# Attention forward of a memory-segment transformer block: softmax sums moved into the score banks, V's far heads copied straight from PSUM, and a reordered store of V and P

## The chip, the cores and the metric

One core of a Trainium2 chip. The metric is device time in microseconds (us), median of several runs. Engines by their names in the profile: PE (TensorE: matmuls; its weight loads are PEld), ACT (ScalarE), DVE (VectorE), POOL (GpSimd) and SP (SyncE, which here issues DMAs; its instruction queue is written SPq).

## The reference

The kernel computes the output of a transformer block and all of its gradients. The part that matters here is the forward of the attention with memory: 2048 rows of 512 are cut into 64 segments of 32 rows, and each segment is attended together with 8 memory rows, which are the first 8 output rows of the segment before. So the 64 steps are sequential.

```python
for s in range(n_seg):
    xs = x[:, s * seg_len:(s + 1) * seg_len, :].copy()
    h = jnp.concatenate([mem, xs], axis=1)
    q = jnp.einsum('btd,dhe->bhte', h, Wq)
    k = jnp.einsum('btd,dhe->bhte', h, Wk)
    v = jnp.einsum('btd,dhe->bhte', h, Wv)
    scores = jnp.einsum('bhqe,bhke->bhqk', q, k) * scale
    scores = jnp.where(mask[None, None], scores, -1000000000.0)
    p = _softmax(scores, axis=-1)
    o = jnp.einsum('bhqk,bhke->bhqe', p, v)
    o = jnp.einsum('bhte,hed->btd', o, Wo)
    mem = o[:, :M, :].copy()
    outs.append(o[:, M:, :])
```

There are 32 heads of 128. After the attention come a gated feed-forward part and the backward of everything, for which the forward stores Q, K, V, the normalised P and the head outputs O of every step.

## The kernel before

The forward is `phase2`, a Python loop over `s` that is unrolled into one program; `s4 = s % 4`. Its instructions are written in order, and `self.pin` keeps that order on each engine, so what an engine does next is the order of the text.

The loop treats 32 rows per step: the 8 memory rows and the first 24 rows of the segment. The last 8 rows of four segments together (the *tails*) are projected as one block of 32 rows, ahead of time (`b_pieces`: RBk, RBq, RBv), and stored at s4 = 1 (RBk) and 2 (RBq). One step runs so:

- Projections of K, Q and V (`col_pass`, L255): each in two halves of 16 heads. Four column groups of TensorE work at once, so the result of a half lies as 128 partitions (4 x 32 rows) by 512: the heads 24 to 31 in partitions 96 to 127. They are copied out of PSUM to RA (L61 on ACT, L63 on DVE). `turns` transposes K and Q by TensorE to the layout kT, qT.
- V has to go to the *head layout* Vst: 11 groups of 3 heads, 32 rows each in partitions 0 to 95, tail rows in 96 to 119 (`v_tails`, by DMA from RBv). GpSimd copies partitions 0 to 95 of each half (L794, L797). The heads of partitions 96 to 127 have to move to other partitions: `vshift` (L740) does it with three products with the identity, and DVE copies the result (L743).
- `st_exp`, three parts of 4, 4 and 3 head groups: scores of a group (L715) are added to a mask that `mask_mm` (L664) has put in the bank (pool `pst`, three banks), and ACT takes the exponential of a part into ET (L717).
- `den` (L721) multiplies ET by a column of ones, the softmax sums; the sums of all parts lie in the last quarter of the bank or2. `pv` (L750) multiplies ET by V. `recip` (L726) and `ost` (L759 ACT, L762 DVE) divide, giving Ost. As part 2's product goes to or2 as well, it comes after the reading of the first sums.
- `ott` (L733) transposes Ost by TensorE to OT, `outproj` (L223) multiplies by Wo; the two halves of the sum are split, folded (L240), and the memory columns become the next step's hT (L875), on which its projections of K wait.

Between these, `slots` and `mod_r` hold side work: turning RBk or RBq (s4 = 2, 3), projecting tails, a 128-column piece of the modulation (mostly s4 = 0), the next layernorm tile.

SP issues the stores and two DMA transpositions per step: VTr from Vst (L814), and Pst from ET (L820), each with a single buffer. P is scaled by GpSimd (`norm`, L885), and VT and PS are stored (L887, L888) in the step after, by the call at its very start. Ost and OT are stored to OSR and OT (L858, L869), the rows of K and Q to KST and QST (L589, L590). All go through one queue of SP in the order of the text.

Of the kernel before, what the change touches and what calls it, by code (L numbers as in the profile page):

```python
# [10 lines left out]
ALU = mybir.AluOpType  # L11
# [29 lines left out]
class K:  # L41
# [392 lines left out]
    def phase2(self):  # L434
        nc, tc, cfg, io = self.nc, self.tc, self.cfg, self.io
        D, DC, H, E, L, M, T, G, NS = cfg.D, cfg.DC, cfg.H, cfg.E, cfg.L, cfg.M, cfg.T, cfg.G, cfg.NS
        GW = 128
        NP = 3
        PG = 4
# [8 lines left out]
        with ExitStack() as ctx:  # L448
# [10 lines left out]
            def ps_f32(name):  # L459
                return psp.tile([128, PG, GW], F32, name=name, tag="p")  # L460
# [92 lines left out]
            def part3(t, pi):  # L553
                return t[:, pi * PW:min((pi + 1) * PW, G * GW)].rearrange("p (g x) -> p g x", x=GW)
# [7 lines left out]
            Ws = {"q": Wq, "k": Wk, "v": Wv}  # L562

            def pass_half(x, hf, lhs, rows, eng):
                self.col_pass(psp, Ws[x], hf, lhs, rows, eng)

            def turn_half(rows, hf):
                return self.turn_half(psp, rows, hf)
# [74 lines left out]
            def fill(s4, where):  # L643
                for f in slots.pop((s4, where), []):
                    f()
# [14 lines left out]
            def mask_mm(pi):  # L660

                n = min(PG, G - pi * PG)
                ps = masked[pi] = pst.tile([128, PG, GW], F32, name="st_ps", tag="st")
                nc.tensor.matmul(ps[:, 0:n, 0:120], lhsT=self.ident[:, :], rhs=maskT[:, 0:n, :], start=True, stop=False,  # L664
                                 skip_group_check=True)
# [15 lines left out]
            for s in range(NS):  # L681
# [10 lines left out]
                def proj(x, hf, eng):  # L692
                    pass_half(x, hf, lambda c: hT[:, c, :], RA[x], eng)
                    if hf == 1 and x != "v" and s < NS - 1:
                        rows_out(RA[x], DR[x], s, 1)
# [5 lines left out]
                def turns():  # L701
                    tps = []
                    for x in "kq":
                        for hf in range(2):
                            tps.append((x, hf, ("act", "dve")[hf], turn_half(RA[x], hf)))
                            to_heads(tps[-1][2], XT[x], tps[-1][3][:], 4 * hf, 4, 32, 0, far=False)
                    for x, hf, eng, tp in tps:
                        to_heads(eng, XT[x], tp[:], 4 * hf, 4, 32, 0, own=False)

                def st_exp(pi):  # L710
                    st_ps = masked.pop(pi)
                    n = min(PG, G - pi * PG)
                    for j in range(n):
                        g = pi * PG + j
                        nc.tensor.matmul(st_ps[:, j, 0:120], lhsT=x120(KT, g), rhs=QT[:, g * 120:g * 120 + 120],  # L715
                                         start=False, stop=True, skip_group_check=True)
                    nc.scalar.activation(part3(ET, pi)[:, 0:n, 0:120], st_ps[:, 0:n, 0:120], AF.Exp, scale=cfg.scale)  # L717

                def den(pi, ps):
                    for g in range(pi * PG, min(pi * PG + PG, G)):  # L720
                        nc.tensor.matmul(ps[:, PG - 1, g:g + 1], lhsT=ET[:, g * GW:(g + 1) * GW], rhs=self.ones[:, 0:1],  # L721
                                         start=True, stop=True)

                def recip(a, b, ps):
                    a, b = a * PG, min(b * PG, G)
                    nc.vector.reciprocal(rden[:, a:b], ps[0:120, PG - 1, a:b])  # L726

                def transposes_part(src, pi, w=GW):
                    ps = ps_b16("tps")
# [3 lines left out]
                        nc.tensor.transpose(ps[:, j, :], src[:, g * w:g * w + GW], self.ident[:, :])  # L733
                    return ps[:, 0:n, :], n

                def vshift():
                    sh = ps_f32("sh_ps")
                    shf = sh[:].rearrange("p g x -> p (g x)")
                    for hl in range(3):
                        nc.tensor.matmul(shf[32 * hl:32 * hl + 32, 0:384], lhsT=self.ident[96:128, 96:128],  # L740
                                         rhs=RA["v"][96:128, 384 * hl:384 * hl + 384], start=True, stop=True,
                                         tile_position=(96, 32 * hl))
                    nc.vector.tensor_copy(Vst[0:96, 1024:1408], shf[0:96, 0:384])  # L743

                def pv(pi, or_ps=None):
                    or_ps = or_ps or ps_f32("or_ps")
                    n = min(PG, G - pi * PG)
                    for j in range(n):
                        g = pi * PG + j
                        nc.tensor.matmul(or_ps[:, j, :], lhsT=ET[:, g * GW:(g + 1) * GW], rhs=Vst[:, g * GW:(g + 1) * GW],  # L750
                                         start=True, stop=True)
                    return or_ps

                def ost(pi, or_ps, eng):
                    n = min(PG, G - pi * PG)
                    if eng == "act":
                        for j in range(n):
                            g = pi * PG + j
                            nc.scalar.activation(Ost[0:120, g * GW:(g + 1) * GW], or_ps[0:120, j, :], AF.Copy,  # L759
                                                 scale=rden[:, g:g + 1])  # L760
                        return
                    nc.vector.tensor_tensor(part3(Ost, pi)[0:120, 0:n, :], or_ps[0:120, 0:n, :],  # L762
                                            rden[:, pi * PG:pi * PG + n].unsqueeze(2).to_broadcast([120, n, 128]), op=ALU.mult)

                def ott(pi):
                    ps, n = transposes_part(Ost, pi)
                    self.evac("dve" if pi == 1 else "act", part3(OT, pi)[:, 0:n, :], ps)

                def outproj():
                    ps = psp.tile([128, 256], F32, name="at_ps", tag="p")  # L770
# [3 lines left out]
                        self.pair_mm(ps, [OT[:, off(h):off(h) + 32] for h in hs], [Wo[:, h, :] for h in hs], n, H // 2)  # L774
                    return ps

                if s < NS - 1 and norms:
                    norms.pop()()
                proj("k", 0, "dve")
                proj("k", 1, "act")  # L780
                if s == NS - 1:
                    nc.gpsimd.dma_start(self.w_gate, io["B_w_gate"].rearrange("(c p) f -> p c f", p=128))
                    norms.pop()()
                if s == 0:
                    for f in firsts["k"]:
                        f()
# [5 lines left out]
                    tails_in("kq", 0)  # L792
                proj("v", 0, "dve")
                nc.gpsimd.tensor_copy(Vst[0:96, 0:512], RA["v"][0:96, 0:512])  # L794
                turns()
                proj("v", 1, "dve")
                nc.gpsimd.tensor_copy(Vst[0:96, 512:1024], RA["v"][0:96, 512:1024])  # L797
                if s == 0:
                    for f in firsts["v"]:
                        f()  # L800
# [7 lines left out]
                    late_rows()  # L808
                st_exp(0)
                st_exp(1)  # L810
                vshift()
                st_exp(2)
                if s < NS - 1:
                    nc.sync.dma_start(VTr[:], Vst[:, :], transpose=True)  # L814
                or2 = ps_f32("or_ps")
                den(0, or2)
                or0 = pv(0)
                Pst = sb2.tile([128, G, 128], BF16, name="Pst", bufs=1)
                if s < NS - 1:
# [1 line left out]
                else:  # L821
                    nc.gpsimd.dma_start(self.w_up, io["B_w_up"].rearrange("(c p) f -> p c f", p=128))
                    nc.gpsimd.dma_start(self.w_down, io["B_w_down"].rearrange("(fc p) d -> p fc d", p=128))
                den(1, or2)
                or1 = pv(1)
                recip(0, 2, or2)
                ost(0, or0, "dve")
                ost(1, or1, "act")
                pv(2, or2)
                den(2, or2)  # L830
                recip(2, 3, or2)
                ost(2, or2, "dve")
                more = list(range(NP)) if s + 1 < NS else []
                turned = bool(slots.get((s4, "turn"))) or bool(mod_r)
                mod_row = mod_r.pop()() if mod_r else None
                if s + 1 in mod_at:
                    load, products = self.mod_rest(psp, sb2, mod_at.index(s + 1))
                    load()
                    mod_r.append(products)
                fill(s4, "turn")  # L840
                if s4 == 3:
                    p1(s // nseg_t + P1_AHEAD, 4)
                    turned = True
                if more and not turned:
                    mask_mm(more.pop(0))
                    mask_mm(more.pop(0))
                ott(0)
                if len(more) > 1:
                    mask_mm(more.pop(0))
                ott(1)  # L850
                if len(more) > 1:
                    mask_mm(more.pop(0))
                ott(2)
                if more:
                    mask_mm(more.pop(0))
                self.pop_later()
                self.pop_later()
                nc.sync.dma_start(self.OSR[s], gl3(Ost))  # L858
# [25 lines left out]
                def norm(s=s, Pst=Pst, rden=rden):  # L884
                    nc.gpsimd.tensor_tensor(Pst[0:120, :, :], Pst[0:120, :, :],  # L885
                                            rden[:, :].unsqueeze(2).to_broadcast([120, G, 128]), op=ALU.mult)
                    nc.sync.dma_start(self.VT[s], VTr[:])  # L887
                    nc.sync.dma_start(self.PS[s], Pst[:])  # L888

                if s < NS - 1:  # L890
                    norms.append(norm)
# [1246 lines left out]
```

The softmax here doesn't subtract the row's maximum and nothing guards it: scores larger than these inputs give would overflow.

## Time and profile before

| What | Value |
|---|---|
| Time, median of 3 runs | 3098.13 us (3097.36 to 3100.67) |
| Profiled run | 3093.9 us |
| First and last exponential of the forward (L717) | 52.4 and 988.8 us |
| Steps of the forward | 64 |
| Softmax sums (L721), product with V (L750), each | 704 instructions |
| Shift products (L740) | 192 of 332 ns |
| Copy of the shifted V (L743) | 64 of 554 ns |
| Product on P (L885) | 63 of 2533 ns |

The forward is the first third of the span. The page's groups mix the phases: they rank costs over the whole kernel, in which the backward and the weight gradients take two thirds. So the forward is read from timelines of single steps. In a timeline each row is a run of like instructions: start, length from the first start to the last end, engine, line, output and inputs, count, and in brackets the idle time of the engine before it with what ended that. TensorE's products overlap in its pipeline, so the lengths of its rows add up to more than the time.

### The profile page before, as it was taken

The page shows a single profiled execution, that of the slowest core. Times are in us where ns is not written, and L with a number is a line of the kernel's source. Part 1 is how long each engine was busy: PE and PEld are TensorE (multiplying, and loading weights), DVE is VectorE, ACT ScalarE, POOL GpSimd, SP SyncE. Part 2 cuts the span into 40 slices and gives each one's busy share as a digit, 9 for nine tenths or more (in the row PEclk, how much of TensorE's full clock was granted, in tenths as well). Part 3 has the DMA queues.
Part 4 walks back from the last instruction along what each step waited for, and adds up shares of the span by engine and source line. Part 5 has one row for each costly group of instructions (what it writes and reads, how often), then busy time and mean ns, then how long its engine had stood idle before and what let it go on. Part 6 is the DMA issues. An engine that isn't in the chain of part 4 may idle for free.

```text
span 3093.9 us, 106049 instructions
## 1 busy us (share of the span) xinstructions
PE 2997.4 (97%) x43769; PEld 1835.7 (59%) x43845; DVE 1628.3 (53%) x3799; ACT 1269.5 (41%) x3056; POOL 1378.6 (45%) x2958
## 2 busy tenths in 40 slices
PE   5999999999999899989999999999999999999999
PEld 3666666666665444445577777777777754445454
DVE  4556656665555788742255555555555642322221
ACT  2555555555555433322255555555555530111011
POOL 3666766666766222211244444444444422333322
PEclk8999999999999899999999999999999999999999
DMA  9887788788788799997599999999999998666574
GB/s 299 217 213 203 205 206 216 201 213 211 206 201 255 200 231 232 224 284 247 170 239 243 245 243 244 239 248 244 244 240 245 245 271 279 195 201 220 190 237 148
DMA packets 845944, 703.54 MB, mean 227 GB/s; under 512 B 544306, under 2 KB 717906, under 8 KB 845076
## 3 DMA queue, kind: packets, MB, share of 16 engines
q1 hardware_dynamic: 714148, 486.69, 62.3%
q0 software_dynamic: 60656, 148.64, 14.9%
q10 hardware_dynamic: 70656, 61.41, 6.4%
q8 instruction: 345, 5.65, 0.8%
q14 instruction: 139, 1.14, 0.1%
HBM read 294.93 MB, written 276.35 MB: 185 GB/s over the span
## 4 chain that ended last, share of the span: by engine, by line
PE 90%; DMA 4%; DVE 3%; issue 1%; POOL 1%; ACT 1%; SPq 0%; another core or an unknown queue 0%; DVEq 0%; POOLq 0%; ACTq 0%
PE pass_ps L255 18%; PE gps L1928 13%; PE dh_ps L215 8%; PE g_ps L1590 6%; PE gps5o L1942 4%; PE at_ps L223 4%; PE dhq_ps L223 4%; PE gps L1277 3%; PE mm L1121 3%; PE dh_tps L215 3%; PE turn_ps L264 2%; PE dp_ps L1569 2%; PE tps L1502 2%; PE tps L733 2%; PE mm L1081 2%; DVE RA0v L63 1%
## 5 line engine op out<-in xcount | busy, mean ns | idle before, releaser
L1928 PE MATMUL gps<-rows,hrows 128*128 128x512 bf16 (+2 forms) x2124 | 415.6, 355 | 1.9
L1928 PEld LDWEIGHTS <-hrows 128*128 128x128 bf16 x2160 | 211.2, 98 | 204.6
L255 PEld LDWEIGHTS <-hT 128*32 128x32 bf16 x6144 | 158.2, 97 | 161.3 <-issue 1.9
L1634 POOL COPY dOst<-RAd 96x512 bf16<-96x512 bf16 x128 | 75.4, 612 | 312.2 <-DVE RAd L63 312.2
L63 DVE CAST ot<-gps 128x512 bf16<-128x512 f32 (+3 forms) x76 | 48.1, 633 | 274.8 <-PE gps L1928 185.8
L1932 POOL DMA_DIRECT2D out_dram<-ot x108 | 81.3, 753 | 248.9 <-DVE ot L63 136.5
L61 ACT ACTIVATE ot<-gps 128x512 bf16<-128x512 f32 (+3 forms) x75 | 41.3, 551 | 349.5 <-PE gps L1928 221.7
L885 POOL TENSOR_TENSOR Pst<-Pst,rden 120x1408 bf16<-120x1408 bf16 x63 | 159.6, 2533 | 43.8 <-issue 28.4
L61 ACT ACTIVATE dVT<-g_ps 128x512 bf16<-128x512 f32 (+1 forms) x192 | 109.5, 570 | 95.3 <-PE g_ps L1590 95.0
L63 DVE CAST RA0v<-pass_ps 128x512 bf16<-128x512 f32 x128 | 88.5, 692 | 89.4 <-PE pass_ps L255 85.5
L215 PE MATMUL dh_ps<-WvT,dVT 128*32 128x512 bf16 x2048 | 133.4, 380 | 0.2 <-DVE RBd L63 0.2
L255 PE MATMUL pass_ps<-Wv,hT 128*32 128x512 bf16 x2048 | 133.3, 380 | 0.0
L1942 PE MATMUL gps5o<-WoT,rows 128*128 128x512 bf16 x580 | 127.8, 379 | 3.9 <-DMA rows<-OSR 3.2
L255 PE MATMUL pass_ps<-Wk,hT 128*32 128x512 bf16 x2048 | 123.3, 383 | 1.5 <-ACT hT L875 1.1
L1579 DVE SCALAR_TENSOR_TENSOR dS<-dp_ps,Pst_l 128x512 bf16<-128x512 f32 (+1 forms) x192 | 112.1, 640 | 22.1 <-PE dp_ps L1577 22.1
L223 PE MATMUL at_ps<-Wo,OT 128*32 128x256 bf16 x4096 | 123.5, 273 | 0.1
L255 PE MATMUL pass_ps<-WoT,dyT 128*32 128x256 bf16 (+1 forms) x3072 | 122.4, 308 | 0.9 <-ACT dyT L1708 0.9
L223 PE MATMUL dhq_ps<-WqT,dQT 128*32 128x256 bf16 x4096 | 122.9, 273 | 0.0
L215 PE MATMUL dh_ps<-WkT,dKT 128*32 128x512 bf16 x2048 | 122.2, 380 | 0.0
L255 PE MATMUL pass_ps<-Wq,hT 128*32 128x512 bf16 x2048 | 121.6, 379 | 0.0
L223 PEld LDWEIGHTS <-dQT 128*32 128x32 bf16 x4096 | 109.6, 97 | 15.9
L717 ACT ACTIVATE ET<-st_ps 128x480 bf16<-128x480 f32 (+1 forms) x192 | 96.0, 535 | 42.6 <-ACT qT L61 34.7
(419 smaller groups left out, 7082.2 us busy)
## 6 DMA issues: line engine op xcount, KB each, us to landing
OSR<-Ost SPq DMA_DIRECT2D x64, 352.0 KB
OT<-OT SPq DMA_DIRECT2D x64, 352.0 KB
VT<-VTr SPq DMA_DIRECT2D x64, 352.0 KB
PS<-Pst SPq DMA_DIRECT2D x64, 352.0 KB
OT_l<-OT SPq DMA_DIRECT2D x64, 352.0 KB
Pst_l<-PS SPq DMA_DIRECT2D x64, 352.0 KB
VT_l<-VT SPq DMA_DIRECT2D x64, 352.0 KB
DVR<-rows_x POOLq DMA_DIRECT2D x64, 352.0 KB, 6.4
```

Of the source, the lines that this page charges most:

```text
L61: return nc.scalar.activation(out, in_, AF.Copy)
L63: return nc.vector.tensor_copy(out, in_)
L215: self.nc.tensor.matmul(ps[32 * j:32 * j + 32, :], lhsT=lhsT, rhs=w, start=(n < 4), stop=(n >= total - 4), tile_position=(0, 32 * j))
L223: nc.tensor.matmul(ps[32 * j:32 * j + 32, :], lhsT=x[k], rhs=w[k][:, 256 * d:256 * d + 256], start=(n == 0), stop=(n == total - 1), tile_p ...
L255: self.nc.tensor.matmul(ps[32 * j:32 * j + 32, :], lhsT=lhs(c), rhs=rhs, start=(c == 0), stop=(c == DC - 1), tile_position=(0, 32 * j))
L717: nc.scalar.activation(part3(ET, pi)[:, 0:n, 0:120], st_ps[:, 0:n, 0:120], AF.Exp, scale=cfg.scale)
L885: nc.gpsimd.tensor_tensor(Pst[0:120, :, :], Pst[0:120, :, :], rden[:, :].unsqueeze(2).to_broadcast([120, G, 128]), op=ALU.mult)
L1121: nc.tensor.matmul(hp[:], lhsT=xT[:, fc, :], rhs=wT[:, fc, :], start=(n == 0), stop=(n == 2 * FC - 1))
L1579: nc.vector.scalar_tensor_tensor(out=part3(dS, pi), in0=ps[:, 0:n, :], scalar=cfg.scale, in1=part3(Pst, pi), op0=ALU.mult, op1=ALU.mult)
L1590: nc.tensor.matmul(ps[:, j, :], lhsT=lh[:, g * GW:(g + 1) * GW], rhs=rh[:, g * GW:(g + 1) * GW], start=True, stop=True)
L1928: nc.tensor.matmul(ps[:, 0:ng * E], lhsT=hrows[:, tp_, c * 128:(c + 1) * 128], rhs=rows[:, tp_, 0:ng * E], start=(tp_ == 0), stop=(tp_ == ...
L1942: nc.tensor.matmul(pss[gg][:], lhsT=src[0][:, src[1], gg * E:(gg + 1) * E], rhs=dyrows[:, tp_, :], start=(tp_ == order[0]), stop=(tp_ == o ...
```

## The change

It touches the body of the forward step only.

1. The softmax sums go to unused columns (120 and on) of the score banks, `sts`, so that or2 holds a product alone, and each part has a reciprocal of its own. The next step's mask in that bank comes after the reading of the sums.
2. `vshift` goes. The second half of V is not copied to RA but from PSUM straight to Vst by DVE, and `far` copies the heads of partitions 96 to 127 in four pieces: 384 wide (ACT, before the exponentials), 256 (DVE), 128 and 256 (ACT, after the exponentials).
3. GpSimd's product on P comes after its copy of the first half of V; VT is stored after the rows of K and Q, and PS (`ps_store`) after the issue of the transposition of V.
4. The turn of the tails and the modulation product move from behind the products with V to behind the scores.
5. `ost` of part 0 is split in halves; OT parts 0 and 2 are copied by DVE and part 1 by ACT (before: 0 and 2 ACT, 1 DVE); masks and transposes change places.

It is meant to take work and waits out of TensorE's order between the scores and the output projection.

```diff
-                def den(pi, ps):
+                def den(pi):
                     for g in range(pi * PG, min(pi * PG + PG, G)):
-                        nc.tensor.matmul(ps[:, PG - 1, g:g + 1], lhsT=ET[:, g * GW:(g + 1) * GW], rhs=self.ones[:, 0:1],
+                        j = 120 + g - pi * PG
+                        nc.tensor.matmul(sts[pi][:, 0, j:j + 1], lhsT=ET[:, g * GW:(g + 1) * GW], rhs=self.ones[:, 0:1],
                                          start=True, stop=True)
...
-                def vshift():
...
+                def far(src, o, eng, lo=None):
+
+                    lo = o and 512 if lo is None else lo
+                    hi = min(384 * (lo // 384) + 384, 512 * (lo // 512) + 512)
+                    hl = lo // 384
+                    self.evac(eng, Vst[32 * hl:32 * hl + 32, 1024 + lo - 384 * hl:1024 + hi - 384 * hl],
+                              src[96:128, lo - o:hi - o])
...
-                if s < NS - 1 and norms:
-                    norms.pop()()
                 proj("k", 0, "dve")
                 proj("k", 1, "act")
...
                 proj("v", 0, "dve")
                 nc.gpsimd.tensor_copy(Vst[0:96, 0:512], RA["v"][0:96, 0:512])
+                ps_store = norms.pop()() if norms else None
                 turns()
-                proj("v", 1, "dve")
-                nc.gpsimd.tensor_copy(Vst[0:96, 512:1024], RA["v"][0:96, 512:1024])
+                v1 = pass_half("v", 1, lambda c: hT[:, c, :], None, None)
+                far(RA["v"], 0, "act")
+                self.evac("dve", Vst[0:96, 512:1024], v1[0:96, :])
+                far(v1, 512, "dve")
...
                 st_exp(0)
                 st_exp(1)
-                vshift()
                 st_exp(2)
+                far(RA["v"], 0, "act", 384)
+                far(v1, 512, "act", 768)
                 if s < NS - 1:
                     nc.sync.dma_start(VTr[:], Vst[:, :], transpose=True)
-                or2 = ps_f32("or_ps")
-                den(0, or2)
+                if ps_store:
+                    ps_store()
...
+                fill(s4, "turn")
+                den(0)
                 or0 = pv(0)
                 Pst = sb2.tile([128, G, 128], BF16, name="Pst", bufs=1)
                 if s < NS - 1:
...
-                den(1, or2)
+                recip(0)
+                ost(0, or0, "dve", 0, 2)
+                den(1)
                 or1 = pv(1)
-                recip(0, 2, or2)
-                ost(0, or0, "dve")
+                recip(1)
                 ost(1, or1, "act")
-                pv(2, or2)
-                den(2, or2)
-                recip(2, 3, or2)
-                ost(2, or2, "dve")
...
+                ost(0, or0, "dve", 2, 4)
                 if s4 == 3:
                     p1(s // nseg_t + P1_AHEAD, 4)
...
+                den(2)
+                or2 = pv(2)
+                recip(2)
+                ost(2, or2, "dve")
                 if more:
                     mask_mm(more.pop(0))
+                ott(0, "dve")()
+                while more:
+                    mask_mm(more.pop(0))
+                o1 = ott(1, "act")
+                o2 = ott(2, "dve")
+                o1()
+                o2()
...
                     nc.sync.dma_start(self.VT[s], VTr[:])
-                    nc.sync.dma_start(self.PS[s], Pst[:])
+                    return lambda: nc.sync.dma_start(self.PS[s], Pst[:])
```

## The prediction

> **What bounds the kernel now.** I read the page's busy line and its chain first. TensorE is busy 97% of the span and owns 90% of the chain.
>
> ```profile
> PE 2997.4 (97%) x43769; PEld 1835.7 (59%) x43845; DVE 1628.3 (53%) x3799; ACT 1269.5 (41%) x3056; POOL 1378.6 (45%) x2958
> ...
> PE 90%; DMA 4%; DVE 3%; issue 1%; POOL 1%; ACT 1%; SPq 0%; another core or an unknown queue 0%; DVEq 0%; POOLq 0%; ACTq 0%
> ```
>
> A busy PE is not a PE at its peak, so I then read TensorE's timeline over one forward step. Columns: start, length, line, output and inputs, count.
>
> ```profile
> 603.95 0.59 PE L715 MATMUL st_ps<-qT,kT 128*128 128x120 bf16 x8
> 604.47 0.74 PE L740 MATMUL sh_ps<-RA0v,ident 32*32 32x384 bf16 x3
> 605.15 0.33 PE L715 MATMUL st_ps<-qT,kT 128*128 128x120 bf16 x3
> ...
> 605.74 0.77 PE L750 MATMUL or_ps<-Vst,ET 128*128 128x128 bf16 x7
> ...
> 606.91 1.02 PE L733 MATMUL tps<-ident,Ost 128*128 128x128 bf16 x11
> ...
> 608.13 0.73 PE L223 MATMUL at_ps<-Wo,OT 128*32 128x256 bf16 x20
> ```
>
> From the first score product to the first output projection, 603.95 to 608.13, pass 4.18 us, though the products between are short. The rest of the step, 608.13 to the next scores at 618.54, is 10.41 us of back-to-back passes that the change leaves alone. By s % 4 the first part takes 4.63 (0: 588.91 to 593.54, it holds the modulation product), 4.18 (1), 4.30 (2: 500.01 to 504.31, turn of RBk; 4.56 at 618.54) and 4.51 us (3: 633.51 to 638.02, turn of RBq and p1tp). Four steps: 17.6 + 4 x 10.41 = 59.3 us; 16 such groups are the forward.
>
> The weight-load timeline shows where TensorE waits inside that part (bracket: idle before, releaser), and ScalarE's timeline what it waits for:
>
> ```profile
> 604.88 0.09 PEld L740 LDWEIGHTS <-ident 32*32 32x32 bf16 x1 [0.32 <-issue]
> ...
> 606.90 0.42 PEld L733 LDWEIGHTS <-Ost 128*128 128x128 bf16 x7 [0.39 <-DVE Ost L762]
> ```
> ```profile
> 604.41 1.63 ACT L717 ACTIVATE ET<-st_ps 128x480 bf16<-128x480 f32 x3 [0.55 <-ACT qT L61]
> 606.29 1.14 ACT L759 ACTIVATE Ost<-or_ps,rden 120x128 bf16<-120x128 f32 x4 [0.25 <-PE or_ps L750]
> 607.48 1.04 ACT L61 ACTIVATE OT<-tps 128x512 bf16<-128x512 bf16 x2
> ```
>
> TensorE waits for the evacuation of V (604.13 to 604.83 on VectorE), then for the normalised output Ost. Last I read the DMA queue that SyncE feeds, because the change reorders it:
>
> ```profile
> 605.88 1.44 SPq L814 DMA_TRANSPOSE VTr<-Vst  x1
> 607.43 1.50 SPq L820 DMA_TRANSPOSE Pst<-ET  x1
> ...
> 612.99 1.92 SPq L594 DMA_DIRECT2D KST<-RBk  x3
> 614.95 1.83 SPq L597 DMA_DIRECT2D KST<-RBk  x3
> 616.83 0.45 SPq L887 DMA_DIRECT2D VT<-VTr  x1
> 617.39 0.36 SPq L888 DMA_DIRECT2D PS<-Pst  x1
> ...
> 620.58 1.52 SPq L814 DMA_TRANSPOSE VTr<-Vst  x1
> ```
> ```profile
> 642.41 2.54 POOL L885 TENSOR_TENSOR Pst<-Pst,rden 120x1408 bf16<-120x1408 bf16 x1 [1.23 <-DMA Pst<-ET]
> ```
> ```profile
> 606.80:611.00 4.20, 4.18 (x99) 3.08 (x98) 2.97 (x10) 2.06 (x6) 4.03 (x9) 1.00 1.29 209
> 617.80:622.00 4.20, 4.07 (x67) 2.77 (x59) 3.28 (x11) 2.99 (x12) 2.83 (x6) 1.00 0.90 309
> ...
> 627.20:629.20 2.00, 2.00 (x44) 0.98 (x40) 0.69 (x1) 0.74 (x2) 2.00 (x5) 1.00 1.07 425
> ```
>
> The reader is to see three things. The stores of V and P (VT, PS) are issued ahead of the next step's row stores, so when the next transposition of V is issued (620.58) its target has long been written out. The two transpositions follow each other without a wait. And the last two columns of the windows (DMA share, GB/s) say the DMA engines are full while these transfers run: two transpositions take 4.2 us (606.8 to 611.0), four row and tile stores of 1.2 MB 4.2 us, OSR and OT 2.0 us.
>
> **What the Trainium skill says.** "DMA: Bandwidth & Descriptors", Anatomy of one DMA (told for the GpSimd path; that it holds for SyncE is my reading): each DMA pays about 2.0 us whatever its size, mostly between the last byte and the semaphore. The trace agrees in kind: the transposition of P issued at 637.12, behind that of V, releases GpSimd only at 642.41. The same page, Two DMAs through the same engine are not ordered: a dependent DMA is issued only after the first one's semaphore; sharing a queue is no substitute. So a transposition into a buffer that is still being stored waits a whole landing. "SBUF — State Buffer", Who interferes with whom: VectorE with at most one SBUF input outside its two-port modes does not contend with GpSimd. The 2.53 us product on P (L885) already runs beside PSUM casts here (613.25, cast at 0.69 us as elsewhere), so moving it beside others costs nothing.
>
> **The change, part by part.** I take the plain step and keep the clock of the trace.
>
> *Removed.* Three shift products (L740) and TensorE's wait for the V cast; one VectorE copy (0.55 us), one GpSimd copy (0.61). The scores then run through to about 604.55.
>
> *Added on ScalarE.* Three copies of 32 partitions. A copy follows the next at its width's pace: 128x384 starts 0.39 to 0.45 us apart, 128x96 about 0.13. The first (384 wide) fits the 0.55 us idle before the exponential. No row shows a copy out of SBUF; I take the PSUM pace. The exponentials start at 604.41, 604.88 and, no longer held by late scores, 605.35, ending 605.82; before, they ended 606.04. The other two copies end about 606.25.
>
> *VectorE.* The V cast goes straight to Vst (0.69, ends 604.83), plus a 256-wide copy (0.42, between the 0.55 of 384 and smaller), ends 605.2. The sums lie in the score banks, so the reciprocals come as each part is ready: 605.5, 606.1, 606.55; the halved product 0.42 us each, the last part 0.56, ending 607.25; then OT part 0 (0.42) until 607.65.
>
> *TensorE.* Sums and products follow each exponential; the third product waits for ScalarE's last copy, 606.3. Turn (0.47) and modulation product (0.55) move into the wait for the first exponential, 604.55 to 605.05, and hide there but for about 0.05. Masks and transposes of Ost end by 607.55, and the projection starts when OT part 0 is there: about 607.70, or 3.75 us after the scores; 3.85 where the modulation product and eight fold products stand (s % 4 = 0). Four steps: 15.1 against 17.6, so TensorE alone would win **2.5 us a group, 40 us in all**.
>
> *The queue.* This is what I think decides. The new order per step is KST, QST, VT, transposition of V, PS, transposition of P, OSR, OT. VT now goes out just ahead of the transposition that overwrites VTr, and PS just ahead of the one that overwrites Pst (one buffer each). Each pair is a landing that nothing covers while SyncE's queue stands. Behind it are OSR, OT and the next rows; and the exponential of the next step waits for the transposition of P to land, as that reads ET. The longest chain from one transposition of V to the next, with transpositions at 2.1 us (half of 4.2), 352 KB at 1.0 (half of 2.0), KST and QST 1.8 (528 KB at 309 GB/s is 1.7) and 2.0 for a landing: 2.1 + 1.0 + 2.0 + 2.1 + 2.0 + 1.8 + 1.0 + 2.0 = **14.0 us**. In the steps with stores of RBk or RBq (s % 4 = 1, 2) the issues set it: 5.1 to P's landing, then 1.5 + 0.5 + 0.4 + 3.8 (612.99 to 616.78) + 1.2 + 1.1 = 8.5 of issues, then VT 1.0 + about 1.3 (its setup is behind the rows): 15.9. With 0.4 for the loads of x and w_mod and 0.2 a step for stalls such as the pair at 622.0 that took 5.2 us instead of 4.2, a group is 2 x 14.0 + 2 x 15.9 + 0.4 + 0.8 = 61.0. TensorE's group would be 56.7, so the backlog grows until the exponential waits for it, and the queue becomes the pace. Against 59.3 that is **+1.7 us a group**. Two groups pass at TensorE's pace before the backlog is full (2 x -2.6), 14 at the queue's (14 x 1.7 = 24): +19, **3117 us**.
>
> Low end of the queue: landings of 1.5 us and no stalls: 13.0 and 14.9, group 56.2, under TensorE's. High end: transpositions of 2.6 (half of 5.2, one of them in the chain of the RB steps): 15.0 and 16.4, group 64.0, +61 us.
>
> **The rivals.** *TensorE's gain comes through:* landings are short or covered, the queue keeps up, and the step ends on VectorE and ScalarE as worked out: 3058; with a wait of some tenths at s % 4 = 0, up to 3090. For it: the queue has idle time in steps without RB stores (603.5 to 605.9). Against: two bare landings. I take 3064 as its time. *A draw:* the queue's group comes out near 59.3: 3097. *Forecast:* the queue sets the pace, 3105 to 3170. GpSimd as the new bound I leave out: its v_tails issues (six of 0.5 us) end about 609, ten microseconds ahead of the product that needs them.
>
> **How the numbers follow.** Forecast 0.55, gain 0.33, draw 0.12. The range takes in the larger part of the gain and the queue's high end with a few more stalls: 3064 to 3168; about one in ten is left out on each side. Faster 0.33, same 0.12, slower 0.55.
>
> **What would show it.** Right: ScalarE's ET waits for DMA Pst<-ET for a microsecond or more in steps with s % 4 = 3 and 0; SyncE's transposition of V starts over a microsecond after Vst is complete; yet the score-to-projection part is 3.7 to 3.9 us where no wait stands. Wrong: no such waits and a group under 58 us (the gain), or a part that stays over 4.1 us because ScalarE's four Ost copies end later than 607.5 (then TensorE's side was mis-sized).

## The result: 2.8% slower, and the profile after

| | Before | After |
|---|---|---|
| Time, median | 3097.74 us (3095.40 to 3100.67) | 3182.68 us (3176.28 to 3192.35) |
| After over before, 95% interval | | 1.0276 [1.0248, 1.0304] |

The change costs 85 us. The direction was forecast, the size was not: 3117 was predicted, with a range up to 3168. From the ratios below one execution is left out, a single one of x4_sbuf_copies_to_pool that took 5966 us.

The page of after, its busy line and its chain:

```profile
PE 2997.2 (94%) x43577; PEld 1850.9 (58%) x43653; DVE 1641.4 (52%) x3991; ACT 1312.9 (41%) x3184; POOL 1340.0 (42%) x2894
...
PE 59%; DMA 5%; issue 4%; POOL 2%; ACT 1%; DVE 1%; SPq 1%; another core or an unknown queue 0%; ACTq 0%; POOLq 0%; DVEq 0%
```

TensorE's busy time equals that of before only by coincidence. The kernel with the old store order (e1 below) has the same products as after and keeps TensorE busy for 2970.1 us; x2 to x5, which have them too, for 2967.1 to 2983.0. So of the 82 us between e1 and after, some 14 to 30 are products that take longer, and the rest is standing. The fall of its share of the chain from 90% to 59% must not be read as the loss. e1, which runs within 0.2% of the kernel before, has 61% there. The chain is one path followed back, and a small shift sends it another way.

Where TensorE stands shows in the waits of the forward (100 to 1080 us; columns: us in total, times, longest). First some rows of all engines, then SyncE's queue alone:

```profile
...
POOL Pst L887 <- DMA Pst<-ET: 89.5, 39, 5.6
PEld L724 <- ACT ET L719: 66.3, 46, 5.1
...
ACT ET L719 <- DMA Pst<-ET: 59.6, 30, 4.6
PE st_ps L724 <- ACT ET L719: 58.6, 46, 4.9
```
```profile
SPq L832 <- DMA PS<-Pst: 154.4, 60, 4.0
SPq L818 <- DMA VT<-VTr: 153.4, 50, 4.9
```

The two lines of SyncE are the two landings that the forecast named: the transposition of P stands 2.6 us on average (154.4 / 60) for the store of the old Pst, that of V 3.1 us (153.4 / 50) for the store of the old VTr. What follows is the other list: the exponential (ACT ET) may not overwrite ET until its transposition has landed, and TensorE's softmax sums (L724) wait for the exponential: 58.6 us, against 5.9 in e1. That is most of the standing.

Why products take longer shows in the windows view. Behind the busy times of the five engines it has the granted clock of TensorE, then the DMA share and GB/s. The first row is most of the forward, the others a stretch of one late step (s % 4 = 0):

```profile
75.00:970.00 895.00, 809.44 (x15076) 522.44 (x15068) 498.76 (x1400) 468.75 (x1267) 531.82 (x1161) 0.97 0.72 190
697.50:701.60 4.10, 2.78 (x47) 2.28 (x44) 2.23 (x8) 3.00 (x8) 2.55 (x2) 1.00 0.99 314
701.70:705.00 3.30, 3.12 (x43) 2.50 (x44) 2.19 (x7) 1.37 (x5) 3.17 (x7) 0.50 0.67 223
```

In before and in e1 the clock is 1.00 from 75 to 970 us. In after it is 0.50 in 16 stretches, 61 us together, and the transposes of Ost at s % 4 = 0 take 275 ns on average instead of 226 (e1). At half clock 61 us hold at most 31 us less of TensorE's work, an estimate that fits those 14 to 30. As e1 has the same products, the lower clock comes with the late stores. That it comes from TensorE's standing is likely but was not tested.

The timeline of SyncE's queue over one step with stores of RBk and the step before it, the counterpart of the one shown for before:

```profile
655.19 1.42 SPq L818 DMA_TRANSPOSE VTr<-Vst  x1
656.73 0.50 SPq L890 DMA_DIRECT2D PS<-Pst  x1
660.24 1.62 SPq L832 DMA_TRANSPOSE Pst<-ET  x1
...
663.05 1.92 SPq L594 DMA_DIRECT2D KST<-RBk  x3
665.02 1.83 SPq L597 DMA_DIRECT2D KST<-RBk  x3
...
668.83 0.44 SPq L889 DMA_DIRECT2D VT<-VTr  x1
673.13 1.41 SPq L818 DMA_TRANSPOSE VTr<-Vst  x1
```

From one transposition of V to the next pass 17.94 us (655.19 to 673.13). They are 5.05 to the end of PS's landing (660.24), 8.59 of issues (to 668.83) and 4.30 of waiting for VT to land. In the step with RBq it is 17.81 (673.13 to 690.94). In steps without such stores it is 13.59 (641.60 to 655.19) and 13.77 (690.94 to 704.71). Over the whole forward the medians are 18.4 with RBk, 17.5 with RBq, 14.0 and 14.4 without. TensorE's step, a little under 15 us, covers the short ones, but not the long ones. The delay falls due in the next two steps, s % 4 = 3 and 0: there stand 28 of the 30 waits of the exponential, 57.4 of 59.6 us. A step with s % 4 = 3, all engines, some rows of the timeline:

```profile
682.03 1.40 ACT L719 ACTIVATE ET<-st_ps 128x480 bf16<-128x480 f32 x3 [0.51 <-DMA Pst<-ET]
...
684.80 0.42 DVE L764 TENSOR_TENSOR Ost<-or_ps,rden 120x256 bf16<-120x256 f32 x1 [1.58 <-DMA OSR<-Ost]
...
685.69 0.40 PE L736 MATMUL tps<-ident,Ost 128*128 128x128 bf16 x4 [0.95 <-DVE Ost L764]
```

The exponential is half a microsecond late for the landing of P. Then comes a wait that the forecast did not list. VectorE stands 1.58 us until the last step's Ost has been stored, as that store (OSR) is behind the transposition of P in the same queue. TensorE then stands for VectorE. This second wait is rare: it comes in 3 of the 64 steps, 4.8 us in all.

The times from the first score product to the first output projection, from the starts of the scores (L715 before, L717 after) and of L223 over the 64 steps, in us. The rest of the step stayed at 10.41 in every kernel here.

| Median by s % 4 | 0 | 1 | 2 | 3 | Mean period of four steps |
|---|---|---|---|---|---|
| before | 4.63 | 4.18 | 4.29 | 4.52 | 59.3 |
| after | 8.06 | 4.26 | 4.20 | 6.13 | 64.5 |

Sixteen groups at 5.2 us more are 83 us: this is nearly the whole loss of 85.

### The profile page after: what moved, and what is told of

The parts are those of the page before. It is cut to its first block, busy times and chain, and to the rows that moved or that the text cites. A ratio compares the mean times of both kernels' runs of the same rounds, so it can differ in the third digit from the quotient of the medians.

```text
span 3182.0 us, 106036 instructions
## 1 busy us (share of the span) xinstructions
PE 2997.2 (94%) x43577; PEld 1850.9 (58%) x43653; DVE 1641.4 (52%) x3991; ACT 1312.9 (41%) x3184; POOL 1340.0 (42%) x2894
## 4 chain that ended last, share of the span: by engine, by line
PE 59%; DMA 5%; issue 4%; POOL 2%; ACT 1%; DVE 1%; SPq 1%; another core or an unknown queue 0%; ACTq 0%; POOLq 0%; DVEq 0%
PE gps L1930 8%; PE dh_ps L215 7%; PE g_ps L1592 6%; PE pass_ps L255 5%; PE gps5o L1944 4%; PE dhq_ps L223 4%; PE gps L1279 3%; PE dh_tps L215 3%; PE mm L1123 3%; PE dp_ps L1571 2%; PE tps L1504 2%; PE mm L1083 2%; PE mm L1056 1%; PE mm L1098 1%; PE mm L1060 1%
## 5 line engine op out<-in xcount | busy, mean ns | idle before, releaser
L794 POOL COPY Vst<-RA0v 96x512 bf16<-96x512 bf16 x64 | 39.1, 611 | 291.3 <-DVE RA0v L63 286.9
L223 PE MATMUL at_ps<-Wo,OT 128*32 128x256 bf16 x4096 | 129.5, 281 | 4.8 <-ACT OT L61 4.7
L223 PE MATMUL dhq_ps<-WqT,dQT 128*32 128x256 bf16 x4096 | 122.9, 273 | 0.0
L223 PEld LDWEIGHTS <-dQT 128*32 128x32 bf16 x4096 | 109.6, 97 | 15.9
L223 PEld LDWEIGHTS <-OT 128*32 128x32 bf16 x4096 | 106.8, 99 | 17.8 <-issue 6.0
```

The lines of the kernel that those rows point to most:

```text
L223: nc.tensor.matmul(ps[32 * j:32 * j + 32, :], lhsT=x[k], rhs=w[k][:, 256 * d:256 * d + 256], start=(n == 0), stop=(n == total - 1), tile_p ...
```

## Experiments

Theory A: the late stores of VT and PS put two bare landings in SyncE's queue, and this is all of the loss. Rival B: GpSimd's product, behind the copy of V, now frees Pst and V too late. A further question was why TensorE's side, forecast to win 40 us, shows 4.20 us in a step without any wait.

### The old store order, and the new one alone

**e1_old_store_order**: the changed kernel with product and stores where they were.

```diff
+                if s < NS - 1 and norms:
+                    norms.pop()()()
                 proj("k", 0, "dve")
...
-                ps_store = norms.pop()() if norms else None
...
-                if ps_store:
-                    ps_store()
```

> The changed kernel, but the product on P by GpSimd and the stores of VT and PS at the very start of the step, as before; all else as changed. Queue theory (two bare landings in SyncE's queue set the pace): both landings lie under the projections again, a group of four steps falls from 64.5 us to TensorE's own pace, 58.5 to 59.3, so 3085 to 3100 us in all; SyncE's waits for PS and VT (154 and 153 us in the changed kernel) fall under 30 each. Rival A (ScalarE's added copies and the new order of products lengthen the step): the time stays over 3150. Rival B (GpSimd's later product delays the tail rows of V): also back to about 3095, so this run does not part B from the queue.

Measured: 3100.26 us against 3097.37, ratio 1.0012 [1.0003, 1.002]. The exponential's wait for the transposition of P is gone from the list. The medians by s % 4 are 4.87, 4.26, 4.20 and 4.35: 17.68 for four steps, against 17.62 before. So all of the loss is in part 3, and parts 1, 2, 4 and 5 together win nothing.

**e2_new_store_order_alone**: the kernel before with part 3 alone (the opposite edit).

> The kernel before, with part 3 of the change alone: GpSimd's product behind its copy of the first half of V, VT stored after the rows of K and Q, PS after the issue of the transposition of V. Queue theory: the loss is all here, 3165 to 3195 us, and the exponential waits for the transposition of P in steps 3 and 0 of a group. Rival A: 3095 to 3110, since nothing that lengthens the step is in it. Rival B: slow too.

Measured: 3199.33, ratio 1.0334 [1.0306, 1.0361], 4 us above the expected range. The waits of SyncE's queue and of the other engines:

```profile
SPq L820 <- DMA PS<-Pst: 183.4, 60, 4.7
SPq L812 <- DMA VT<-VTr: 142.1, 55, 4.0
```
```profile
PE or_ps L750 <- POOL Vst L795: 62.3, 60, 1.9
...
ACT ET L717 <- DMA Pst<-ET: 15.3, 10, 2.4
```

The landings are there again. But the kernel before still needs GpSimd's copy of the second half of V (L795), and this now stands behind the 2.53 us product, so the product with V waits about 1.0 us a step (62.3 / 60). The run confirms that part 3 is costly by itself. Its size is not that of the queue alone.

### GpSimd's product back at the start, stores late

**e5_product_early_stores_late**: the changed kernel with the product on P issued at the start of the step, the stores left late.

```diff
+                ps_store = norms.pop()() if norms else None
                 proj("k", 0, "dve")
...
-                ps_store = norms.pop()() if norms else None
+                if vts:
+                    vts.pop()()
...
-                    nc.sync.dma_start(self.VT[s], VTr[:])
...
+                    vts.append(lambda s=s: nc.sync.dma_start(self.VT[s], VTr[:]))
```

> The changed kernel with the product on P back at the start of GpSimd's step, but VT and PS stored as late as the change does it. Queue theory: nothing gained, 3170 to 3195. Rival B (the place of the product on GpSimd is what costs): 3095 or so, and SyncE's waits for the tail rows Vst<-RBv (24 us) gone.

Measured: 3197.4, ratio 1.0327 [1.0305, 1.0348]. Rival B as the whole cause falls: with the product early, the time isn't regained. The page's waits say why it even gets worse.

```profile
POOL Pst L889 <- DMA Pst<-ET: 283.3, 60, 9.9
...
PE or_ps L752 <- POOL Vst L795: 57.7, 34, 2.3
```

The late landing of P is now waited for by GpSimd, with the copy of V queued behind it. Given late stores, putting the product behind the copy helps. e4 below bounds B from the other side: it leaves the product where the change put it.

### One landing at a time

**e4_vt_early**: the changed kernel, VT alone stored at the start of the step, ahead of KST and QST.

```diff
+                if vts:
+                    vts.pop()()
                 proj("k", 0, "dve")
...
-                    nc.sync.dma_start(self.VT[s], VTr[:])
...
+                    vts.append(lambda s=s: nc.sync.dma_start(self.VT[s], VTr[:]))
```

> The changed kernel with one edit: VT is stored at the start of the step, ahead of the rows of K and Q; the product on P and PS stay where the change put them. Queue theory: one of the two bare landings (3.1 us on average, 50 waits) is gone; the chain between two transpositions of V drops from 13.7 and 17.9 us to about 11.5 and 13.5, under TensorE's step of 14.6, so the whole loss goes: 3085 to 3105. If each landing costs its own share whatever the pace of TensorE: half of the loss, about 3140. Rival B: unchanged, about 3180.

Measured: 3115.77, ratio 1.0057 [1.004, 1.0073], about 10 us above what was expected. The wait of the transposition of V fell from 153.4 to 16.9 us, that of the transposition of P rose to 195.8, and the exponential's fell to 8.7:

```profile
SPq L834 <- DMA PS<-Pst: 195.8, 60, 5.2
SPq L820 <- DMA VT<-VTr: 16.9, 28, 2.5
```

With one landing off the chain, 67 of the 85 us come back. The other one, 3.3 us in each step (195.8 / 60), and the late product together cost 15.5 us against e1.

**x6_ps_early**: its complement, product and PS at the start, VT late.

```diff
-                    nc.sync.dma_start(self.VT[s], VTr[:])
-                    return lambda: nc.sync.dma_start(self.PS[s], Pst[:])
+                    nc.sync.dma_start(self.PS[s], Pst[:])
+                    return lambda: nc.sync.dma_start(self.VT[s], VTr[:])
```

> The complement of e4_vt_early: the changed kernel with the product on P and the store of PS at the start of the step, and VT alone stored late, behind QST and ahead of the transposition of V. Theory (each of the two bare landings alone fits under TensorE's pace, both in series don't): the chain in the steps with row stores falls from 17.8 by one landing of 3.0 to 3.5 us to about 14.5, and the time is 3100 to 3125. Rival (the landing of VT, delayed behind the row stores to 4.3 us, is what costs, that of PS is harmless): 3150 to 3185.

Measured: 3147.66, ratio 1.0158 [1.0143, 1.0173]: between the two expectations, 2 us below the rival's, and no clean test. PS can go out only when the product is done, and the queue now stands for that (second line below), in place of the landing of PS.

```profile
SPq L820 <- DMA VT<-VTr: 178.1, 56, 5.1
SPq L889 <- POOL Pst L887: 84.9, 33, 2.7
```

### The stores of RBk and RBq behind VT

**x1_rb_behind_vt** touches neither landing. It takes the six row stores of a block of tails, 3.8 us of issues, from ahead of VT to behind it, so that they fill VT's landing.

```diff
-                        rows_out(RBt[x], DR[x], t * nseg_t, nseg_t)
+                        rb_stores.append(lambda: rows_out(RBt[x], DR[x], t * nseg_t, nseg_t))
...
                 ps_store = norms.pop()() if norms else None
+                while rb_stores:
+                    rb_stores.pop(0)()
```

> The changed kernel with one edit: the stores of RBk and RBq (six each, about 3.8 us of issues, steps s % 4 = 1 and 2) are held back and issued in the next step behind the store of VT, so that VT no longer stands behind them and their issues cover its landing. Theory (the long chain is that of the two steps with these stores: landing of PS, then 8.5 us of issues, then a landing of VT that took 4.3 us[...]): the chain between two transpositions of V in these steps falls from 17.8 to 13.6 to 14.5 us, below TensorE's 14.6 to 15.3, ET's waits for the transposition of P nearly vanish, and the time is 3098 to 3115 us. Rival (two bare landings a step cost the time by themselves, wherever the rows are issued, or the rows then delay the transposition and PS by as much): the chain stays over 16 us and the time is 3150 to 3185.

Measured: 3122.07, ratio 1.0078 [1.0063, 1.0094]. The timeline of SyncE's queue:

```profile
637.95 1.77 SPq L821 DMA_TRANSPOSE VTr<-Vst  x1
...
648.65 0.34 SPq L892 DMA_DIRECT2D VT<-VTr  x1
649.05 1.90 SPq L594 DMA_DIRECT2D QST<-RBq  x3
651.00 1.83 SPq L597 DMA_DIRECT2D QST<-RBq  x3
653.20 1.55 SPq L821 DMA_TRANSPOSE VTr<-Vst  x1
```

The transposition follows the rows 0.37 us after their last issue ends (652.83): they cover VT's landing. The chain that holds the stores of rows is 15.25 us here (637.95 to 653.20) instead of 17.8 to 17.9; the medians are 15.5 with RBk and 15.3 with RBq, against 18.4 and 17.5. 61 of the 85 us are back with both landings still in the queue (the transposition of V waits 67.0 in all, that of P 173.6). So the theory's mechanism holds, but the chain was forecast at 13.6 to 14.5 and stays at or over TensorE's pace. That fits a time 7 us above the expected range: waits of the exponential stay at 19.0 us in all, in 11 steps, and the part at s % 4 = 3 and 0 has means of 5.12 and 5.76 against medians of 4.46 and 5.09, so some groups still stall.

### TensorE's side: what keeps the clean step at 4.20 us

All of these start from e1, without late stores.

**x5_no_second_copies** leaves out ScalarE's two copies behind the exponentials, so that some columns of V are not filled.

> The changed kernel with the old store order (e1_old_store_order, 3100.3 us) and ScalarE's two copies behind the exponentials left out (so parts of V's last columns are not filled): the bound of what they cost. Theory: as in x2, the part falls from 4.20 to 3.8 to 3.9 us, at s % 4 = 0 from 4.87 to about 4.5, and the time to 3072 to 3086. Rival: no change, 3096 to 3102.

Measured: 3083.63, ratio 0.9966 [0.9954, 0.9979]. The part falls from 4.20 to 3.91, at s % 4 = 0 from 4.87 to 4.71 where 4.5 was expected, and the time by 16.6 us from e1. The two copies cost about 0.29 us in a clean step.

**x2_copies_off_act**: those out of SBUF go to GpSimd, the one out of PSUM moves ahead of the exponentials.

```diff
-                far(RA["v"], 0, "act")
+                far(RA["v"], 0, "pool")
+                far(RA["v"], 0, "pool", 384)
+                far(v1, 512, "act", 768)
                 self.evac("dve", Vst[0:96, 512:1024], v1[0:96, :])
...
-                far(RA["v"], 0, "act", 384)
-                far(v1, 512, "act", 768)
```

> The changed kernel with the store order of the kernel before (as in e1_old_store_order, 3100.3 us), and ScalarE relieved behind the exponentials: both 32-partition copies of rows of V out of SBUF (384 and 128 wide) go to GpSimd, and the 256-wide copy out of PSUM takes the place of the 384-wide one ahead of the exponentials. Theory (the TensorE gain did not come because the two copies behind the exponentials cost ScalarE 0.73 us unoverlapped, which holds the third product and the four Ost copies): the four Ost copies start about 0.36 us earlier (now bound by the reciprocal), the score-to-projection part falls from 4.20 to 3.8 to 3.9 us, and the time by 4 x 0.36 x 16 = 23 us to 3072 to 3086. Rival (TensorE's own passes and the bank of the projection set the part): it stays at 4.1 to 4.2 and the time at 3096 to 3102. Second rival: GpSimd's two copies arrive late and the third product waits for them: over 3102.

Measured: 3097.92, ratio 1.0006 [0.9998, 1.0014], part 4.16. Nothing came of it, and neither rival had named the reason. The waits and VectorE's timeline show it:

```profile
DVE Vst L63 <- ACT Vst L61: 40.1, 61, 0.8
```
```profile
587.99 1.15 DVE L63 CAST Vst<-pass_ps 96x512 bf16<-96x512 f32 x2 [0.76 <-ACT Vst L61]
```

VectorE's cast and ScalarE's copy read the same PSUM tile, and the cast, second in the text, starts only when the copy is done: 0.66 us a step (40.1 / 61). With it the reciprocals come late. The exponentials, now behind a copy, start a little late as well, 0.52 us after the scores instead of 0.47 (medians). So the four Ost copies start 2.58 us after the scores, hardly earlier than e1's 2.62.

**x3_copies_off_act_ott_swap** is x2 with VectorE and ScalarE exchanged in the copies of OT parts 1 and 2.

```diff
-                o1 = ott(1, "act")
-                o2 = ott(2, "dve")
+                o1 = ott(1, "dve")
+                o2 = ott(2, "act")
```

> x2_copies_off_act, and VectorE and ScalarE change places in the last two evacuations of the turned output (OT part 1 on VectorE, part 2 on ScalarE), since at s % 4 = 0 the projection reuses the PSUM bank that ScalarE's copy of part 1 (0.60 us) frees last. Theory: at s % 4 = 0 the part falls by a further 0.15 to 0.25 us and elsewhere by 0 to 0.1: 2 to 8 us below x2, the best of all, 3066 to 3082. Rival (the bank is not what is waited for, or part 2 on ScalarE now comes late for the last products): the same as x2 or up to 10 us slower.

Measured: 3096.9, ratio 1.0002 [0.9994, 1.001]. A miss: at s % 4 = 0 the part is 4.89 (x2: 4.83), and TensorE still stands there for a ScalarE copy of OT, now that of part 2. The reading that the projection waits for the bank of part 1 was wrong or incomplete. What it waits for there is left open.

**x4_sbuf_copies_to_pool**: only the two copies out of SBUF move to GpSimd. That out of PSUM stays behind the exponentials.

```diff
-                far(RA["v"], 0, "act")
+                far(RA["v"], 0, "pool")
+                far(RA["v"], 0, "pool", 384)
...
-                far(RA["v"], 0, "act", 384)
                 far(v1, 512, "act", 768)
```

> The changed kernel with the old store order (e1_old_store_order, 3100.3 us), and the two 32-partition copies of rows of V out of SBUF (384 and 128 wide) on GpSimd; the 256-wide copy out of PSUM stays on ScalarE behind the exponentials. In x2_copies_off_act that copy stood first, and VectorE's cast of V out of the same PSUM tile waited for it (0.66 us a step), which gave the gain back. Theory: without that wait the four Ost copies start about 0.36 us earlier than in e1 and the exponentials about 0.1, so the part falls from 4.20 to 3.75 to 3.9 us and the time to 3072 to 3084, below both kernels and at or below x5 (3083.6). Rival (VectorE's cast and its second copy of V then hold the third product or the first Ost product, or GpSimd's copies come late): the part stays over 4.05 and the time is 3092 to 3100.

Measured: 3087.73, ratio to before 0.9967 [0.9954, 0.998]: faster than both kernels by a little. The median stands 4 us above the expected range; the part is 3.92, just over its upper end. The five executions in the ratio took 3083.8 to 3090.85 us.

ScalarE's timeline in a clean step (s % 4 = 2), first of after, then of x4:

```profile
729.55 0.52 ACT L61 ACTIVATE Vst<-RA0v 32x384 bf16<-32x384 bf16 x1
730.08 1.40 ACT L719 ACTIVATE ET<-st_ps 128x480 bf16<-128x480 f32 x3
731.50 0.31 ACT L61 ACTIVATE Vst<-RA0v 32x128 bf16<-32x128 bf16 x1
731.83 0.38 ACT L61 ACTIVATE Vst<-pass_ps 32x256 bf16<-32x256 f32 x1
732.24 1.14 ACT L761 ACTIVATE Ost<-or_ps,rden 120x128 bf16<-120x128 f32 x4
```
```profile
553.59 1.40 ACT L719 ACTIVATE ET<-st_ps 128x480 bf16<-128x480 f32 x3 [0.55 <-ACT qT L61]
...
555.01 0.38 ACT L61 ACTIVATE Vst<-pass_ps 32x256 bf16<-32x256 f32 x1
...
555.45 1.14 ACT L761 ACTIVATE Ost<-or_ps,rden 120x128 bf16<-120x128 f32 x4
```

Compare start and length. The three exponentials pass in 1.40 us. They start 0.47 apart, though one of 128 x 480 takes 0.57, so neighbours overlap by 0.10. The SBUF copy starts when the last of them has ended (731.48) and ends at 731.81, before the next starts at 731.83. It overlaps with neither. Nor does the PSUM copy: in x4 it stands right behind the exponentials and also starts only after their end (555.01 against 554.99). From the start of the exponentials to that of the Ost copies pass 2.16 us in after and 1.86 in x4, a difference of 0.30, and the part falls from 4.20 to 3.92. x5, without the PSUM copy too, starts its Ost copies no earlier (2.33 us after the scores in both, medians). So beyond the SBUF copy nothing was to be had here: the reciprocal, which ends at 555.37 in this step of x4, is next.

## Why the prediction was right in direction and wrong in size

**Right.** The queue decides, through the wait named: the exponential waits for the landing of P at s % 4 = 3 and 0. The step without row stores was put at 14.0 us and measured 13.6 and 13.8. In part this is luck: in the first of them PS has landed after 4.29 us (641.60 to 645.89) instead of 5.1, VT takes 3.47 instead of 3.0, and the 5.83 between, forecast as 5.9 of data, are issues back to back. In the steps with row stores, the landing of PS (5.1 forecast, 5.05 and 5.67 measured) and the issues (8.5 forecast, 8.59 and 8.36 measured) hold as well. "DMA: Bandwidth & Descriptors" of the Trainium skill (Two DMAs through the same engine are not ordered) fits what the queue does: the transposition of P is held 60 times until the store of its buffer is complete, that of V 50 times, 154.4 and 153.4 us in all.

**Wrong: the last term of the chain with row stores.** It was "VT 1.0 + about 1.3 (its setup is behind the rows)", 2.3 us in all. It measured 4.30 and, in the step with RBq, 3.78 (687.16 to 690.94); over all groups the medians are 4.19 and 3.79. So the rows shorten nothing: VT takes at least as long there as in a step without them (3.47 from 651.72 to 655.19; medians 3.54 and 3.44). The chain is 17.8 to 17.9 instead of 15.9. By the medians the term is 1.9 and 1.5 us too small. In 16 groups that makes 3.4 x 16 = 54 us, most of the 66 between +19 and +85. That the landing of VT together with the rows ahead of it sets the chain is shown by x1. That the rows' data slow that of VT was only argued. The windows view over such a wait (last two columns: DMA share, GB/s) shows that the engines, taken together, were far from full:

```profile
666.90:673.10 6.20, 5.70 (x130) 4.62 (x127) 4.25 (x14) 4.70 (x12) 5.22 (x9) 1.00 0.56 181
```

In the stretches of before that the forecast read, the share was 0.90 to 1.29. So the bandwidth of all engines together isn't short here; the queue waits for single transfers to complete. The share is a mean, though: that a few of the engines were full of rows isn't excluded.

**Wrong: TensorE's side.** The part was put at 3.75 us, "2.5 us a group, 40 in all". It measured 4.20 in the clean step, and e1 shows the gain at nothing. The sentence that fails is "A copy follows the next at its width's pace". That pace was read from copies in a row, which overlap (those of kT and qT by 0.04 to 0.14 us in before). The copies of 32 partitions behind the exponentials overlap with neither neighbour; in x4 that holds for the one out of PSUM too, so the source, of which the forecast was unsure, is not the reason. The two copies behind the exponentials, forecast to end 0.43 us after them (605.82 to 606.25), end 0.73 after (731.48 to 732.21). That is the 0.30 that x4 removes, and with it ScalarE meets the forecast's pace. The sign that the prediction named for this case came: the Ost copies end at 733.38, 3.77 us after the scores at 729.61, where 607.5 was 3.55. The price of a copy of unknown kind was not bounded from both sides. A better bound was to be had: "ScalarE: Activation LUTs" of the Trainium skill (What ACT_TABLE_LOAD costs) gives 186 ns + 0.833 ns an element for such an operation, and an overlap of about 93 ns between neighbours. For 128 and 256 columns this is 0.29 and 0.40 us, an estimate of 0.69 for the two without overlap and 0.50 with one at both sides. The trace has 0.31 and 0.38, no overlap, and 0.02 us of gap ahead of each: 0.73.

A further 0.17 remains in x4 (3.92 against 3.75). Its cause is read from one step and not tested: VectorE is on time, its copy of OT part 0 ending at 556.76, 0.28 ahead of the projection (557.04). TensorE's own order is late: seven transposes of Ost (556.40 to 557.05), some of which need ScalarE's last Ost copy (to 556.59), and the product at_tp stand ahead of the projection. The transposes end 3.93 us after the scores (553.12), where the forecast had 3.60. At s % 4 = 0 the forecast of 3.85 compares with 4.87; TensorE waits there 0.40 us for a copy of OT, and e1 and x3 have not settled why.

**Wrong by omission.** With no TensorE gain, the credit of two groups (5 us) falls away and the queue's pace counts from nearly the first group. The forecast also kept "the clock of the trace": in after that clock is lower in places, and TensorE's products take some 14 to 30 us more. How much of this adds to the time is open, as the queue alone already makes a group of 64.3 us by the medians of its four steps (14.0 + 18.4 + 17.5 + 14.4). The wait of VectorE for the store of Ost (3 steps, 4.8 us) hardly counts.

Not tried: a second buffer for Pst or for VTr, which should take a landing off without touching the order.

## What to carry to other kernels

Storing a single buffer just ahead of the transfer that refills it puts a whole landing into the issuing queue, with all that is queued behind it; the old order hid these 3 to 4 us by issuing the stores ahead of the rows of K and Q. Add up such a queue by step, with the landing measured behind the traffic that really stands ahead of it. And before work moves to an engine with idle time, ask whether it comes between two operations of a chain there: 0.3 us a step on ScalarE took the gain on TensorE's side. With the copies out of SBUF on GpSimd instead (x4), 9 us of gain are left, of the 40 forecast.

## What was not expected of the hardware

- ScalarE's copies of 32 partitions, out of SBUF (32 x 128, 0.31 us) or PSUM (32 x 256, 0.38 us), start 0.02 us after the end of the exponential ahead of them (the first in 60 steps of e1, the second in 61 of x4). Exponentials of 128 x 480 overlap with the next by 0.10 us, and copies of kT and qT with 128 partitions by up to 0.14. Which property of the small copies does it was not tested. The same SBUF copies on GpSimd take 0.29 (128 wide) and 0.51 us (384 wide); in x4 TensorE waited for them once, 0.2 us.
- Two engines reading one PSUM tile did not do it at once: VectorE stood 0.66 us a step for ScalarE's copy (x2). "PSUM — Partial Sum Buffer" of the Trainium skill (PSUM bank collisions raise a hardware error) lets two engines into one bank at once if they are in different quarters of the partitions, as here (0 to 95, and 96 to 127). The trace agrees that the order comes from the program: in x2 all 64 casts wait for ScalarE's semaphore, in e1 and x4 for TensorE's.
- The store of 352 KB, from issue to the release of the transfer behind it, took 3.4 to 4.2 us (medians of VT by step in after), with a DMA share of 0.56 in the one window read.
- Where TensorE stood for late data, its granted clock fell as well. From 75 to 970 us it was at 0.50 for 61 us in after, 48 in e2, 72 in e5, 27 in x6, 14 in x1 and 7 in e4, and for none in before, e1 and x2 to x5.
